# A retention block with two expert layers on one core: each chunk's attention gathered into one piece, and the weight conversion re-portioned around it

## The chip, the cores and the metric

The kernel runs on one core of one Trainium2 chip. The metric is device time in microseconds (us) of one launch. Three runs of the kernel before gave 1004.82, 1004.98 and 1005.65 us, median 1004.98.

## The reference: what is computed

Inputs are float64 arrays in two expert layers and float32 arrays in the attention; the kernel splits each wide number into a high and a low half and multiplies in three passes.

```python
# attention: batch 4, heads 8, 768 steps, head size 64; gamma is one number per head
for t in range(S):
    state = gamma * state + outer(k[:, :, t], v[:, :, t])
    y[:, :, t] = scale * q[:, :, t] @ state
x = y as (3072, 512)
h = x @ w_in                                   # 512 -> 2048
x = where(h > 0, h, exp(min(h, 0)) - 1) @ w_out  # 2048 -> 512
h = max(x @ w1, x @ w2, x @ w3)                # 512 -> 768
out = h @ w_out2                               # 768 -> 512
```

## The kernel before

**Chunks and blocks.** The 3072 tokens are 24 chunks of 128 (`NCHUNK`); four chunks make one block of 512 tokens (`BLK`, `CB = 4`), so there are six blocks, counted from 0. Six chunks make one sequence (`NCH`): chunks 12 and 18 begin one and need no old state, chunks 17 and 23 end one and need no new state.

**A chunk's attention** has these parts. `scores(c)` (L154): sixteen TensorE (PE) passes into two PSUM tiles `sc`. `mask(c)` (L166): VectorE (DVE) multiplies both by the decay mask into `a`. `mix(c)`, the values: `xo` from the old state and the decayed queries `qd` (L205), then from `a` and v (L209); ScalarE (ACT) copies `xo` to `xh` (L217). `rest(c)` (L222): DVE makes the low half `xl`. `update(c)`: `up` from the decayed keys `kd` and v (L182), then DVE decays the old state into the new one (L189, both operands in SBUF) and adds `up` from PSUM (L192); in a sequence's first chunk it only copies `up` (L187). `prep(c)` makes `qd` (L130) and `kd` (L138), from chunk 8 on by GpSimd (POOL). `qd`, `kd` and `a` have one buffer each from chunk 12 on.

**The first expert layer** runs through `seq`, steps of a block b and a slice f of 128 of the 2048 hidden units. A step issues `h1` of the next slice (12 matmuls into a PSUM tile `hp`, L339), then `o1` of its own (12 matmuls into four `acc` tiles, L371). Behind `hp` stands a chain: ACT exp (L346), ACT relu (L347), DVE max (L348, reads `hp`), ACT cast to `gh` (L349), DVE subtraction to `gl` (L352); `o1` reads `gh` and `gl` one step later. `hp`, `xo`, `up` and `sc` share four PSUM buffers, `ps_h`. After a block's last slice `x2_out` empties `acc` (ACT L403, DVE L405).

**Weight conversion** of the second expert layer is cut into portions by `pump(k)`, which lets the generator `conversion` go on for k credits: DVE L280, L290, L291, L298, L306, L307 and ACT L283, L301 for each half tile, and DVE L427, L430, L435 with ACT L433 for the sums of weights. From step `split` (32) on, `h1` itself pumps 2 credits ahead of L352 and 2 behind it, and each step pumps more at its end.

**The order** on PE, DVE, ACT and SP is the order in which the code issues the work; POOL's is left to a scheduler. In blocks 2 to 4 the step f with f % 4 == 1 issues `values(c)` for the next block's chunk ahead of its `h1`, and the step with f % 4 == 2 issues `following(c)`, the next chunk's scores and mask. These are chunks 12 to 23.

Of the kernel before, what the change touches and what calls it, by code (L numbers as in the profile page):

```python
# [40 lines left out]
def kernel(ctx: ExitStack, tc: tile.TileContext, qkv0, qkv, wa, wb, dmask, qdec, cols, out):  # L41
# [10 lines left out]
    ps_h = ctx.enter_context(tc.tile_pool(name="ps_h", bufs=4, space=bass.MemoryType.PSUM))  # L52
# [21 lines left out]
    CB = BLK // P  # L74
# [70 lines left out]
    def scores(c, pool, tag):  # L145

        if c >= NCHUNK:
            return
        x = raw_t[c]
        sc = sc_t[c] = [pool.tile([P, NPAIR, P], F32, tag=tag, name="sc") for _ in range(2)]  # L150
        for p in range(NPAIR):
            for r in range(2):
                h = slice(r * D, (r + 1) * D)
                nc.tensor.matmul(sc[r][:, p, :], x[h, p, 1, :], x[h, p, 0, :], start=p == 0, stop=p == NPAIR - 1)  # L154

    def mask(c):
        if c >= NCHUNK:
            return
        sc = sc_t.pop(c)
        a = st_t[c][2]  # L160
        if a is None:
            a = at.tile([P, 2, NPAIR, P], F32, tag="a", name="a")
        else:
            a = a.rearrange("t r p i -> t r p i")
        for r in range(2):
            nc.vector.tensor_tensor(  # L166
                out=a[:, r], in0=sc[r], in1=dmask_sb.rearrange("j (p r) i -> j r p i", r=2)[:, r], op=ALU.mult
            )
        a_t[c] = a
# [3 lines left out]
    def update(c, pool, tag):  # L173

        kd = st_t[c][1]
        if c % NCH == NCH - 1:
            return
        v = raw_t[c][:, :, 3, :].rearrange("t p (r d) -> t p r d", r=2)
        up = pool.tile([P, NPAIR, D], F32, tag=tag, name="up")
        for p in range(NPAIR):  # L180
            for r in range(2):
                nc.tensor.matmul(  # L182
                    up[r * D:(r + 1) * D, p, :], kd[:, p, r, :], v[:, p, r, :], start=p == 0, stop=p == NPAIR - 1
                )
        new, old = state[c % 2], state[1 - c % 2]
        if c % NCH == 0:
            nc.vector.tensor_copy(new, up)  # L187
        else:
            nc.vector.tensor_tensor(  # L189
                out=new, in0=old, in1=cols_sb[:, H:H + NPAIR].unsqueeze(2).to_broadcast([P, NPAIR, D]), op=ALU.mult  # L190
            )
            nc.vector.tensor_tensor(out=new, in0=up, in1=new, op=ALU.add)  # L192

    def mix(c, pool, tag, then=None):
        v = raw_t[c][:, :, 3, :].rearrange("t p (r d) -> t p r d", r=2)
        qd = st_t[c][0]
        a = a_t.pop(c)
        xo = xo_t[c] = pool.tile([P, NPAIR, P], F32, tag=tag, name="xo")
        first = True
        if c % NCH != 0:  # L200
            old = state[1 - c % 2]
            for p in range(NPAIR):
                for r in range(2):
                    h = slice(r * D, (r + 1) * D)
                    nc.tensor.matmul(xo[h, p, :], old[h, p, :], qd[h, p, :], start=p == 0, stop=False)  # L205
            first = False
        for p in range(NPAIR):
            for r in range(2):
                nc.tensor.matmul(  # L209
                    xo[r * D:(r + 1) * D, p, :], v[:, p, r, :], a[:, r, p, :],  # L210
                    start=first and p == 0, stop=p == NPAIR - 1,
                )
        if then:
            then(c, pool, tag)
        del raw_t[c], st_t[c]
        b, t0 = divmod(c * P, BLK)
        nc.scalar.copy(x_t[b][0][:, :, t0:t0 + P], xo)  # L217

    def rest(c):
        b, t0 = divmod(c * P, BLK)  # L220
        xh, xl = x_t[b]
        nc.vector.tensor_tensor(  # L222
            out=xl[:, :, t0:t0 + P], in0=xo_t.pop(c), in1=f32(xh[:, :, t0:t0 + P]), op=ALU.subtract
        )
# [95 lines left out]
    NB = NT // BLK  # L320

    def new_x(b):
        x_t[b] = (
            xpool.tile([P, KDM, BLK], F32R, tag="xh", name="xh"),
            xpool.tile([P, KDM, BLK], F32R, tag="xl", name="xl"),
        )
# [159 lines left out]
    def pump(k):  # L486

        credit[0] += k
        while credit[0] > 0:
            credit[0] -= next(pending, 1000000)  # L490
# [111 lines left out]
    def values(c):  # L602

        b = c // CB
        if b not in x_t:
            new_x(b)
        load(c)
        load(c + 1)
        load(c + 2)
        if c + 1 < NCHUNK:  # L610
            prep(c + 1)
        mix(c, ps_h, "h", update)
        rest(c)

    def following(c):
        scores(c + 1, ps_h, "h")
        mask(c + 1)

    def pool(name, bufs, **k):
        return ctx.enter_context(tc.tile_pool(name=name, bufs=bufs, reuse_waits="tile", **k))  # L620
# [158 lines left out]
    for i, (b, f, f0, f1) in enumerate(seq):  # L779
        if i < 2:  # L780
            continue
        if (b, f0) in units:
            done = (units[b, f0] - 1) * CB + f // CB
            if f % CB == 1:
                values(done)
            elif f % CB == 2:
                following(done)
        c = EARLY
        if split - 5 <= i < split - 1 or i == split:
            k = c + min(i - split + 5, 4)  # L790
            scores(k, ps_h, "h")
            mask(k)
        if i == split - 2:
            part_t[b] = []
            for m in range(KDM):
                o = f32(dpool.tile([P, BLK], (I32, F32)[m % 2], tag="tm"[m % 2], name="tm"[m % 2]))
                nc.sync.dma_start(out=o, in_=x2d[m, :, b * BLK:(b + 1) * BLK])
                part_t[b].append(o)
        if i == split - 1:
            o1(b, f, f0, f1)  # L800
            x2_out(b, f0, f1, False)
            h1(*seq[i + 1][:2])
            prep(c + 4)
            continue
        if i == len(seq) - 5:
            pump(100000)
            reopen()
            load_sums(0)
            sums(0)
            for k in XORD:  # L810
                later.append(lambda k=k: split_sum(0, k))
        if i == len(seq) - 4:
            fetch_set(loads[-1][0])
        if i == len(seq) - 3:
            fetch_set(loads[-1][1])
            fetch_set(loads[-1][2])
        if i + 1 == len(seq):
            break
        if i < split and n < 2 * KFF:
            h1(*seq[i + 1][:2], [(cv_high, n)], [(cv_bits, n + 1)] if n + 1 < 2 * KFF else [])  # L820
        elif i >= len(seq) - 5:
            h1(*seq[i + 1][:2], [], [(catch_up, 1)])
        elif i > split:
            h1(*seq[i + 1][:2], [(pump, 2)], [(pump, 2)])
        else:
            h1(*seq[i + 1][:2])
        o1(b, f, f0, f1)
        if f == f1 - 1:
            x2_out(b, f0, f1, f1 < KFF and (b, f0) != (0, 10))
        if i >= len(seq) - 5:  # L830
            catch_up(2)
        elif i > split:
            pump(1 if b < NB - 1 and f % CB in (1, 2) else 4)
        for at_step, k in ((11, c), (8, c + 1), (7, c + 2), (5, c + 3), (2, c + 4)):
            if i == split - at_step:
                load(k)
        if i == split - 7:
            prep(c)
        if split - 5 <= i < split - 1:
            if i == split - 5:  # L840
                new_x(2)
            end(c + i - split + 5)
            rest(c + i - split + 5)
        for at_step, k in ((5, 1), (4, 2), (3, 3)):
            if i == split - at_step:
                prep(c + k)
        if i < split and n < 2 * KFF:
            cv_low(n)
            if n + 1 < 2 * KFF:
                cv_rest(n + 1)  # L850
            n += 1
            if i == 2:
                cv_high(n)
                cv_bits(n + 1)
                cv_low(n)
                cv_rest(n + 1)
                n += 1
        while i < split and done_f < n // 2:
            if done_f >= RES:
                keep(done_f)  # L860
            done_f += 1
        for c, g in ((0, i + 1), (1, i)):
            if g < len(seq):
                b, f = seq[g][:2]
                if b >= 2 and f >= KFF - NRING and b + 1 < NB:
                    fetch(RES + f - (KFF - NRING), c)
                if b == 2 and 1 <= f <= NRING:
                    fetch(RES + f - 1, c)
                if b >= 2 and RES <= f < KFF - NRING:
                    fetch(f + NRING, c)  # L870
# [12 lines left out]
    for v, (s, j) in enumerate(visits):  # L883
# [3 lines left out]
        if 2 <= v < 2 + KF2:  # L887
            f = v - 2
# [88 lines left out]
```

## Time and profile before

| | |
|---|---|
| median of three runs | 1004.98 us |
| the profiled execution's own time | 1005.29 us |
| its span | 1003.5 us |
| PE busy | 984.8 us (98%) |
| DVE busy | 690.7 us (69%) |
| ACT busy | 352.9 us (35%) |
| POOL busy | 35.9 us (4%) |
| granted TensorE clock | 1.00 throughout |

The span is the profiled execution from its first to its last instruction; 1.79 us of its own time lie around it. "Busy" of PE counts a matmul up to its modelled end, so the rows are read by the starts of matmuls. A row of the timeline gives start, length, engine, line, operation, tiles, shape and count; in brackets stands idle time ahead of it and what ended it. PE's records count each attention matmul twice.

### The profile page before, as it was taken

How to read it: one execution, taken by the hardware profiler on the slowest of the kernel's cores; microseconds unless marked ns; L12 is line 12 of the kernel's file. 1: busy time of each engine (PE TensorE's matmuls, PEld its weight loads, DVE VectorE, ACT ScalarE, POOL GpSimd, SP SyncE). 2: the span in 40 equal slices, each digit the busy share in tenths (PEclk: the TensorE clock that was granted, in tenths of full speed). 3: DMA queues.
4: the chain of work that ended last, by engine and by line, in shares of the span. 5: the costliest groups of instructions: out<-in, count | busy, mean ns of one | idle time of the engine just before them, and what ended most of it. 6: DMA issues, size and time to landing. Idle time of an engine off the chain costs nothing.

```text
span 1003.5 us, 14377 instructions
## 1 busy us (share of the span) xinstructions
PE 984.8 (98%) x5684; PEld 848.0 (85%) x5685; DVE 690.7 (69%) x1190; ACT 352.9 (35%) x630; POOL 35.9 (4%) x31
## 2 busy tenths in 40 slices
PE   7989999999999999999999999999999999999998
PEld 5777888777888888888888788999899989989996
DVE  4889989975576776677776743688658827864771
ACT  4546555422434444444434443311301311130110
POOL 0000000120011100001100000000000000000000
PEclk9999999999999999999999999999999999999999
DMA  9723336876538773696428717983355055204601
GB/s 272 202 83 106 104 127 198 277 218 207 179 98 268 262 256 96 230 314 211 157 85 325 282 54 271 373 322 145 105 177 212 1 185 211 98 22 156 253 1 63
DMA packets 75315, 180.78 MB, mean 180 GB/s; under 512 B 5872, under 2 KB 42736, under 8 KB 71024
## 3 DMA queue, kind: packets, MB, share of 16 engines
q1 hardware_dynamic: 73088, 175.92, 51.6%
q10 hardware_dynamic: 2160, 3.94, 1.1%
q8 instruction: 45, 0.74, 0.3%
q14 instruction: 22, 0.18, 0.1%
HBM read 139.20 MB, written 40.63 MB: 179 GB/s over the span
## 4 chain that ended last, share of the span: by engine, by line
PE 86%; DVE 7%; DMA 4%; ACT 2%; issue 1%; SPq 0%; ACTq 0%; DVEq 0%
PE pp L693 26%; PE hp L339 24%; PE acc L371 23%; PE ac L745 10%; DMA x<-in_qkv 2%; DMA raw<-in_wa 1%; PE xo L209 1%; PE sc L154 1%; PE xo L205 1%; DVE gl L352 1%; DVE e L348 1%; DVE part L388 1%; DVE t L298 1%; ACT gh L349 1%; DVE w L307 1%; DVE m L291 1%
## 5 line engine op out<-in xcount | busy, mean ns | idle before, releaser
L693 PE MATMUL pp<-xs,op 128*128 128x384 f32 x1512 | 267.8, 334 | 0.0
L693 PEld LDWEIGHTS pp<-xs,op 128*128 128x128 f32 x1512 | 263.3, 188 | 3.0
L339 PE MATMUL hp<-xh,w 128*128 128x512 f32 x768 | 248.1, 394 | 4.7 <-DVE state L192 2.5
L371 PE MATMUL acc<-gh,w 128*128 128x512 f32 x768 | 193.9, 391 | 3.1 <-ACT w L301 1.7
L339 PEld LDWEIGHTS hp<-xh,w 128*128 128x128 f32 x768 | 143.7, 188 | 38.1 <-ACT w L301 2.4
L371 PEld LDWEIGHTS acc<-gh,w 128*128 128x128 f32 x768 | 143.0, 188 | 36.4 <-ACT w L301 2.6
L348 DVE SCALAR_TENSOR_TENSOR e<-e,hp 128x512 f32<-128x512 f32 x96 | 65.7, 685 | 111.6 <-ACT e L347 111.6
L339 PE MATMUL hp<-xl,w 128*128 128x512 f32 x384 | 141.9, 390 | 0.0
L745 PE MATMUL ac<-w,g 128*128 128x512 f32 x432 | 104.5, 391 | 0.0
L371 PE MATMUL acc<-gl,w 128*128 128x512 f32 x384 | 102.7, 389 | 0.0
L346 ACT ACTIVATE e<-hp 128x512 f32<-128x512 f32 x96 | 57.2, 596 | 103.0 <-PE hp L339 102.9
L745 PEld LDWEIGHTS ac<-w,g 128*128 128x128 f32 x432 | 80.6, 188 | 14.9
L349 ACT CAST gh<-e 128x512 fp32r<-128x512 f32 x96 | 59.7, 622 | 89.0 <-DVE e L348 89.0
L709 ACT COPY u<-pp 128x384 f32<-128x384 f32 x36 | 17.3, 480 | 201.2 <-PE pp L693 140.9
L371 PEld LDWEIGHTS acc<-gl,w 128*128 128x128 f32 x384 | 72.1, 188 | 15.1
L339 PEld LDWEIGHTS hp<-xl,w 128*128 128x128 f32 x384 | 72.1, 188 | 14.4
L352 DVE TENSOR_TENSOR gl<-e,gh 128x512 fp32r<-128x512 f32 x96 | 68.5, 713 | 19.7 <-ACT gh L349 16.9
L701 DVE TENSOR_TENSOR c<-pp,u 128x384 f32<-128x384 f32 x96 | 52.8, 553 | 36.1 <-PE pp L693 35.7
L347 ACT ACTIVATE e<-e 128x512 f32<-128x512 f32 x96 | 60.7, 633 | 3.1
L283 ACT ACTIVATE t<-t 128x512 int32<-128x512 int32 x56 | 35.4, 633 | 54.1 <-DVE t L280 54.1
L301 ACT CAST w<-t 128x512 fp32r<-128x512 f32 x56 | 34.8, 621 | 43.4 <-DVE t L298 40.0
L723 DVE TENSOR_TENSOR h<-h,c 128x768 f32<-128x768 f32 x48 | 45.9, 957 | 1.6
(72 smaller groups left out, 817.1 us busy)
## 6 DMA issues: line engine op xcount, KB each, us to landing
op<-opd SPq DMA_DIRECT2D x24, 1792.0 KB, 7.5
w<-kept SPq DMA_DIRECT2D x56, 512.0 KB, 6.7
raw<-in_wa SPq DMA_DIRECT2D x32, 512.0 KB, 3.7
x<-in_qkv SPq DMA_DIRECT2D x24, 512.0 KB, 6.2
raw<-in_wb SPq DMA_DIRECT2D x24, 512.0 KB, 4.4
x<-in_qkv SPq DMA_DIRECT2D x80, 128.0 KB, 5.3
opd<-w SPq DMA_DIRECT2D x9, 1024.0 KB, 8.0
kept<-w SPq DMA_DIRECT2D x14, 512.0 KB, 5.6
```

The source lines that it names most:

```text
L283: nc.scalar.activation(t, t, ACTF.Relu, scale=8.0, bias=-896.0 * 2 ** 23)
L339: nc.tensor.matmul(hp, w[:, pw, kk * P:(kk + 1) * P], x[px][:, kk, :], start=k == 0, stop=k == len(order) - 1,)
L346: nc.scalar.activation(e, hp, ACTF.Exp)
L347: nc.scalar.activation(e, e, ACTF.Relu, scale=-1.0, bias=1.0)
L348: nc.vector.scalar_tensor_tensor(out=e, in0=e, scalar=-1.0, in1=hp, op0=ALU.mult, op1=ALU.max)
L349: nc.scalar.copy(gh, e)
L352: nc.vector.tensor_tensor(out=gl, in0=e, in1=f32(gh), op=ALU.subtract)
L371: nc.tensor.matmul(acc_t[b][m], w[:, p[0], m * P:(m + 1) * P], g[p[1]], start=f == f0 and p == first, stop=f == f1 - 1 and p == final,)
L693: nc.tensor.matmul(o, ws[i][:, pw, kk * P:(kk + 1) * P], xs[i][:, px, kk, :], start=k == 0, stop=k == 5)
L701: nc.vector.tensor_tensor(out=out, in0=a, in1=c, op=ALU.add)
L723: nc.vector.tensor_tensor(out=h_t[s, p][i], in0=h_t[s, p][i], in1=c[i], op=ALU.max)
L745: nc.tensor.matmul(ac_t[s, m], g[:, px, m * P:(m + 1) * P], wo_t[f][:, pw, :], start=first and i == 0, stop=final and i == 2,)
```

## The change

In `values`, the update stands ahead of the values, the next chunk's scores stand right behind them, and the mask behind `rest`, followed by two credits of conversion. `following` is gone. The credits at a step's end were 4, 1, 1, 4 for f % 4 = 0, 1, 2, 3 and become 0, 3, 4, 4.

```diff
-        mix(c, ps_h, "h", update)
+        update(c, ps_h, "h")
+        mix(c, ps_h, "h")
+        scores(c + 1, ps_h, "h")
         rest(c)
-
-    def following(c):
-        scores(c + 1, ps_h, "h")
         mask(c + 1)
+        pump(2)
...
             if f % CB == 1:
                 values(done)
-            elif f % CB == 2:
-                following(done)
...
         elif i > split:
-            pump(1 if b < NB - 1 and f % CB in (1, 2) else 4)
+            pump((0, 3, 4, 4)[f % CB] if b < NB - 1 else 4)
```

PE, block 2, around chunk 14: `up` is the state's increment, `xo` the values, `sc` the scores of chunk 15, `acc` belongs to `o1` and `hp` to `h1`. Before:

```order
L371 MATMUL acc<-gl,w 128x512 x4
L205 MATMUL xo<-qd,state_93 64x128 x8
L209 MATMUL xo<-a,x 64x128 x8
L182 MATMUL up<-x,kd 64x64 x8
L339 MATMUL hp<-xh,w 128x512
...
L371 MATMUL acc<-gl,w 128x512 x4
L154 MATMUL sc<-x 128x128 x8
L339 MATMUL hp<-xh,w 128x512
```

and now:

```order
L371 MATMUL acc<-gl,w 128x512 x4
L182 MATMUL up<-x,kd 64x64 x8
L205 MATMUL xo<-qd,state_93 64x128 x8
L209 MATMUL xo<-a,x 64x128 x8
L154 MATMUL sc<-x 128x128 x8
L339 MATMUL hp<-xh,w 128x512
```

The update moved ahead of the values, the scores moved one step forward, and the next `hp` is the fifth PSUM tile counted from `up` instead of the second: it takes `up`'s buffer.

DVE, the same place (`t`, `m`, `raw`, `w` are conversion, `e` and `gl` the chain behind `hp`). Before:

```order
L348 SCALAR_TENSOR_TENSOR e<-e,hp 128x512
L430 TENSOR_TENSOR w<-w 128x256
L352 TENSOR_TENSOR gl<-e,gh 128x512
L306 TENSOR_SCALAR t<-t 128x512
L307 SCALAR_TENSOR_TENSOR w<-m,t 128x512
L435 TENSOR_TENSOR w<-w 128x256
L280 TENSOR_SCALAR t<-raw 128x512
L427 TENSOR_TENSOR w<-w 128x256
L189 TENSOR_TENSOR state_92<-state_93,cols_sb 128x256
L192 TENSOR_TENSOR state_92<-up,state_92 128x256
L222 TENSOR_TENSOR xl<-xo,xh 128x4x128
```

and now:

```order
L348 SCALAR_TENSOR_TENSOR e<-e,hp 128x512
L352 TENSOR_TENSOR gl<-e,gh 128x512
L430 TENSOR_TENSOR w<-w 128x256
L435 TENSOR_TENSOR w<-w 128x256
L189 TENSOR_TENSOR state_92<-state_93,cols_sb 128x256
L192 TENSOR_TENSOR state_92<-up,state_92 128x256
L222 TENSOR_TENSOR xl<-xo,xh 128x4x128
L166 TENSOR_TENSOR a<-sc,dmask_sb 128x512 x2
```

Between L348 and L189 there were seven instructions and are now three; the masks follow at once.

POOL, `kd` and `qd` of chunks 13 to 16. Before:

```order
L130 TENSOR_TENSOR qd<-x,qdec_sb 128x512
L138 TENSOR_TENSOR kd<-x,cols_sb 128x512
L130 TENSOR_TENSOR qd<-x,qdec_sb 128x512
L138 TENSOR_TENSOR kd<-x,cols_sb 128x512
L130 TENSOR_TENSOR qd<-x,qdec_sb 128x512
```

and now:

```order
L138 TENSOR_TENSOR kd<-x,cols_sb 128x512 x2
L130 TENSOR_TENSOR qd<-x,qdec_sb 128x512
L138 TENSOR_TENSOR kd<-x,cols_sb 128x512
L130 TENSOR_TENSOR qd<-x,qdec_sb 128x512
L138 TENSOR_TENSOR kd<-x,cols_sb 128x512
```

`kd` of the next chunk, whose buffer the update sets free, now stands ahead of `qd`, whose buffer L205 sets free.

## Rows read from the trace of the kernel before

**Rows 1.** The page, busy time: engine, us, share of the span, instructions.

```profile
PE 984.8 (98%) x5684; PEld 848.0 (85%) x5685; DVE 690.7 (69%) x1190; ACT 352.9 (35%) x630; POOL 35.9 (4%) x31
```

**Rows 2.** Busy time by stretch, blocks 2 to 4: PE, PEld, DVE, ACT, POOL, clock.

```profile
245.00:550.00 305.00, 305.00 (x1848) 248.53 (x1847) 210.72 (x394) 131.24 (x233) 24.56 (x19) 1.00 0.63 209
```

**Rows 3.** Timeline of PE around chunk 14 and the steps behind it.

```profile
303.35 1.09 PE L205 MATMUL xo<-qd,state 64*64 64x128 f32 x16
...
305.86 0.50 PE L339 MATMUL hp<-xh,w 128*128 128x512 f32 x1
...
308.72 1.98 PE L371 MATMUL acc<-gh,w 128*128 128x512 f32 x8
...
311.53 1.16 PE L154 MATMUL sc<-x 64*128 64x128 f32 x16
312.62 0.50 PE L339 MATMUL hp<-xh,w 128*128 128x512 f32 x1
...
318.20 0.39 PE L339 MATMUL hp<-xh,w 128*128 128x512 f32 x1
...
320.92 0.39 PE L371 MATMUL acc<-gh,w 128*128 128x512 f32 x1
```

**Rows 4.** Timeline of PE and DVE at chunk 9, where the update already stands first.

```profile
218.27 0.69 PE L182 MATMUL up<-x,spare 128*64 128x64 f32 x16
...
220.93 1.16 PE L154 MATMUL sc<-x 64*128 64x128 f32 x16
...
222.38 0.42 DVE L192 TENSOR_TENSOR state<-up,state 128x256 f32<-128x256 f32 x1
...
222.86 0.50 PE L339 MATMUL hp<-xh,w 128*128 128x512 f32 x1 [0.77 <-DVE state L192]
```

**Rows 5.** Waits of PE: who, for whom, us in total, times, longest.

```profile
PE hp L339 <- DVE state L192: 2.5, 3, 1.4
```

**Rows 6.** Timeline of DVE, then of POOL, at chunk 8.

```profile
209.17 1.37 DVE L352 TENSOR_TENSOR gl<-e,gh 128x512 fp32r<-128x512 f32 x1
210.46 1.48 DVE L189 TENSOR_TENSOR state<-state,cols_sb 128x256 f32<-128x256 f32 x1
...
208.57 1.42 POOL L138 TENSOR_TENSOR kd<-x,cols_sb 128x512 f32<-128x512 f32 x1 [4.90 <-DMA x<-in_qkv]
209.95 1.71 POOL L130 TENSOR_TENSOR qd<-x,qdec_sb 128x512 f32<-128x512 f32 x1
```

**Rows 7.** Timeline of PE and POOL: `kd` behind an update (chunk 12), `qd` at chunk 9.

```profile
253.66 0.64 PE L182 MATMUL up<-x,kd 128*64 128x64 f32 x16
...
254.44 1.04 POOL L138 TENSOR_TENSOR kd<-x,cols_sb 128x512 f32<-128x512 f32 x1 [1.79 <-PE up L182]
...
220.12 1.27 POOL L130 TENSOR_TENSOR spare<-x,qdec_sb 128x512 f32<-128x512 f32 x1 [8.46 <-PE xo L205]
```

**Rows 8.** Timeline of DVE and ACT in an undisturbed step of block 2.

```profile
322.41 0.69 DVE L348 SCALAR_TENSOR_TENSOR e<-e,hp 128x512 f32<-128x512 f32 x1 [1.46 <-ACT e L347]
...
324.08 0.68 DVE L352 TENSOR_TENSOR gl<-e,gh 128x512 fp32r<-128x512 f32 x1
324.69 0.42 DVE L430 TENSOR_TENSOR w<-w 128x256 f32<-128x256 f32 x1
325.57 0.43 DVE L435 TENSOR_TENSOR w<-w 128x256 fp32r<-128x256 f32 x1 [0.47 <-ACT w L433]
...
323.13 0.62 ACT L349 CAST gh<-e 128x512 fp32r<-128x512 f32 x1 [0.76 <-DVE e L348]
325.13 0.41 ACT L433 CAST w<-w 128x256 fp32r<-128x256 f32 x1 [1.38 <-DVE w L430]
```

**Rows 9.** Timeline of PE and ACT where block 5 begins.

```profile
552.99 0.39 PE L339 MATMUL hp<-xh,w 128*128 128x512 f32 x1
...
556.25 2.10 PE L371 MATMUL acc<-gh,w 128*128 128x512 f32 x8 [0.38 <-ACT w L301]
...
557.38 0.59 ACT L346 ACTIVATE e<-hp 128x512 f32<-128x512 f32 x1
```

## The prediction

> **What bounds the kernel now.** I read the page's busy times first: PE is busy for 984.8 of 1003.5 us [rows 1]. In the table by stretch the part that the change touches, blocks 2 to 4, shows PE busy in all of 305 us at the full clock, while DVE works 211 us and ACT 131 us [rows 2]. So PE's own order of work is the path there: time can be won only by shortening what PE runs, and is lost wherever another engine makes it wait. The third view is PE's timeline, from which two things are read: what a switch between large matmuls and the small ones of attention costs, and which waits PE has where the new order already exists, in chunks 8 to 10.
>
> **What PE saves.** Twelve matmuls of `h1` or `o1` take 320.92 - 318.20 = 2.72 us [rows 3]. The twelve ahead of an attention part take 311.53 - 308.72 = 2.81, those behind one 308.72 - 305.86 = 2.86: leaving costs 0.09, coming back 0.14. Before, a chunk is left and entered twice: 0.09 + 2.51 (303.35 to 305.86, values and update) + 0.14, then 0.09 + 1.09 (311.53 to 312.62, scores) + 0.14 = 4.06 us. In the new order update and values take 220.93 - 218.27 = 2.66 [rows 4], 0.15 more than 2.51, because the inner changes of shape differ. The sum is 0.09 + 2.66 + 1.09 + 0.14 = 3.98. Chunks 13 to 16 and 19 to 22 so save 0.08 each, 0.64. Chunks 12, 17 and 18 lack either values from the state or the update, so inner changes fall away, and they save up to 0.09 + 0.14 = 0.23 each, 0.69. Chunk 23 has no next scores and saves nothing. **PE saves 1.3 us in all**; the bounds are 0.9 (0.08 for all eleven) and 2.5 (0.23 for all).
>
> **What the credits do.** Over blocks 2 to 4 the steps' ends and `values` now hand out 13 credits in four steps instead of 10, and conversion is done when block 4 is, where it used to reach into block 5. DVE has room: 305 - 211 us [rows 2]. At the start of block 5 twelve matmuls take 556.25 - 552.99 = 3.26 instead of 2.72, since ACT casts a weight (L301) ahead of emptying `acc` [rows 9]. With less conversion there **0.5 us** should go; bounds are 0 and 0.54. The conversion's DMAs keep their number and come earlier; SP's x loads stand at the same step, a whole chunk (some 26 us) ahead of use, so I price both at nothing.
>
> **The new wait.** `hp` of the step behind the piece takes the buffer of `up`, which is free when L192 has read it. Behind that matmul all of PE's queue waits. The same layout stands at chunks 8 to 10, and there PE waited for L192 three times out of three, 2.5 us together [rows 5], [rows 4] for one. I count from the piece's first matmul. `hp` is due at 2.66 + 1.09 = 3.75, and starts 0.06 after L192's end (222.80 to 222.86). L192 takes 0.42, its forerunner L189 as long when undisturbed, 0.10 lies between. So L189 must begin by 2.75.
>
> What delays it is POOL. While POOL runs L138 or L130, a DVE instruction whose inputs are all in SBUF stands still: L352 began inside L138 and ended 0.55 after it (210.54 against 209.99); L189 began inside L130 and ended 0.28 after it (211.94 against 211.66) [rows 6]. Undisturbed they take 0.68 [rows 8] and 0.42. So POOL stops one such instruction per operation. In the new order POOL's `kd` stands ahead of its `qd` and begins 0.78 after an update does [rows 7], with the first small matmul's delay 0.83. It takes between 1.04 [rows 7] and 1.42 [rows 6], I take 1.22; `qd` takes 1.27 [rows 7] to 1.71 [rows 6], I take 1.5, the middle in both, as DVE competes in every chunk. POOL is thus in the way from 0.83 to 3.55, just when L189 is due.
>
> Chunk 14 in full: `o1` starts 2.81 ahead of the piece, L348 1.49 after that [rows 3, 8], so at -1.32. L349 starts 0.72 later and takes 0.62, to 0.02; L352 starts at 0.07. L430 follows 0.61 later at 0.68, ACT's L433 at 1.12, L435 at 1.56 [rows 8]. That falls into `kd` (to 2.05), so L435 ends at 2.33. L189 falls into `qd` (to 3.55) and ends at 3.83; L192 runs to 4.35; `hp` starts at 4.41 instead of 3.75: **0.7 us lost**.
>
> The other chunks go by what still stands ahead of L189 at 0.83. With two such instructions (13, 19, 21) both of POOL's operations are used up by them, L189 begins near 3.8 and `hp` is 1.1 late. In 15 they are L290 and the longer L291: 1.3. Chunk 16 has no `kd` to make, but its chain starts late: behind a block's last slice ACT empties `acc` first, and at block 5 L346 began at 557.38 where 552.99 + 2.72 + 0.20 = 555.91 was due [rows 9], 1.5 late. That moves L189 behind `qd` (which begins 1.85 after the piece [rows 4, 7]): 1.1. In 20 L433, L435, L280 and L283 stand behind the copies as well, four operations of about 0.4 with their hand-overs; L346 is 2.5 late and six DVE instructions remain ahead of L189: 2.7. Chunk 22 has no `kd`, and L189 starts near 1.7, ahead of `qd`: 0. Chunks 12, 17, 18 and 23 have no L189. **Sum: 1.1 + 0.7 + 1.3 + 1.1 + 1.1 + 2.7 + 1.1 = 9.1 us.** Bounds: 0, when every L189 begins by 2.75, and about 13, when POOL takes its longer 1.42 and 1.71 (0.4 more in seven chunks, 3) and chunk 15 loses a second wide instruction. Many starts lie within 0.1 us of POOL's, which is why I keep the middle value. The three early pieces, at 0.8 on average, would give 6.7 for eight.
>
> Here the Trainium skill can be weighed (SBUF — State Buffer, "Who interferes with whom"): the side that starts first holds the shared ports for its whole instruction and the other "fully blocks". By that page a stopped DVE instruction would run its whole length after POOL's, 0.42 where the trace shows 0.28; that would add 0.14 in seven chunks, 1.0 us. The measurement decides.
>
> **The sum.** -1.3 - 0.5 + 9.1 = +7.3 us. The profiled execution's own time is 1005.29 (span 1003.5), which gives 1012.6; it lies 0.3 above the median of the runs, 1004.98, so I forecast **1012.3**.
>
> **Rivals.**
> 1. *Nothing is stopped.* If DVE clears its queue early enough that L189 itself is what `kd` stops, it ends near 2.3 and L192 near 2.9, in time. It decides at L435 in chunk 14, which would have to begin before 0.83, 0.7 earlier than reckoned, and likewise elsewhere. For it: the step ahead of `values` now has no credits at its end, and DVE is free for a third of the time. Against it: ACT's cast stands between L430 and L435, and all three early pieces waited. Time: 1005.0 - 1.3 - 0.5 = 1003.2, not slower.
> 2. *Half of it.* The queue is some 0.4 us ahead of my reckoning, so that one instruction fewer is stopped in 13, 15, 19 and 21, each then costing 0.7, and L346 is on time in 16 and 20 (0.3 each): 0.7 x 5 + 0.6 = 4.1. Time: 1004.98 - 1.8 + 4.1 = 1007.3.
> 3. *DVE falls behind.* With 13 credits L346 comes 1.5 late or more in most pieces, as at block 5 [rows 9]; chunks 13 to 16 and 19 to 21 then all cost about what 20 does, 2.7 x 7 = 19. Time: 1022. Against it: only steps that follow a block's end show such lateness so far.
>
> **How the numbers follow.** About 0.2% (2 us) is what a measurement of this kernel can tell from no change. The forecast has 0.60, rival 1 0.14, rival 2 0.14, rival 3 0.12. Rival 1 lies within 0.2% or, with PE's upper bound of 2.5 saved, below it: 0.05 faster and 0.09 the same; rival 2 adds 0.03 to the same. So faster 0.05, same 0.12, slower 0.83. The forecast with its bounds runs from about 1008 to 1016; the range goes down to 1005.0 to take in rival 2 and up to 1017.0 for a mild form of rival 3, and leaves out rival 1.
>
> **What would show it.** Right: PE's waits name L192 behind `hp` in six or seven of chunks 13 to 16 and 19 to 21, each row following a piece; L189 or the instruction ahead of it reads 1.2 to 1.6 us; chunk 20 is the worst; DVE has no conversion in block 5; twelve matmuls at block 5's start take about 2.72. Pieces without a wait run 3.98 from large to large. Wrong: `hp` following `sc` without idle time (rival 1), or waits at `acc` for `gl` and `gh` across blocks 2 to 4 (rival 3).

## The result and the profile after

The changed kernel takes **1015.03 us** in the median (1014.52 to 1015.81), the kernel before on the same chip 1005.32 (1004.82 to 1005.86): a ratio of 1.010, 95% interval 1.0088 to 1.0113. The profiled execution's own time is 1014.52 us, its span 1012.6, which is 9.1 more than before.

The page's busy times, and the line of `h1`'s matmuls among its costliest groups (matmuls, their busy time and mean ns, then the idle time just before them and what ended most of it):

```profile
PE 986.2 (97%) x5685; PEld 850.0 (84%) x5685; DVE 688.5 (68%) x1190; ACT 354.5 (35%) x630; POOL 35.4 (3%) x31
...
L339 PE MATMUL hp<-xh,w 128*128 128x512 f32 x768 | 247.9, 394 | 12.2 <-DVE state L192 9.9
```

Against [rows 1] PE is busy 1.4 us longer and the span is 9.1 longer: most of the loss is idle time of PE. The list of PE's waits of the changed kernel says whom it waited for (in total, times, longest):

```profile
PE hp L339 <- DVE state L192: 9.9, 10, 2.6
```

The three early waits of [rows 5] have become ten. The table by stretch, for blocks 2 to 4 as in [rows 2] and then two microseconds at a time around chunk 20 (columns: stretch, its length, busy us of PE, PEld, DVE, ACT, POOL, the clock, DMA):

```profile
245.00:550.00 305.00, 296.93 (x1808) 242.40 (x1807) 214.35 (x408) 132.98 (x235) 24.77 (x20) 0.99 0.63 213
...
464.00:466.00 2.00, 1.24 (x20) 0.97 (x16) 1.97 (x4) 1.40 (x3) 0.55 (x1) 1.00 0.16 47
466.00:468.00 2.00, 0.12 (x1) 0.12 (x2) 1.86 (x5) 0.00 (x0) 0.00 (x0) 1.00 0.65 178
468.00:470.00 2.00, 2.00 (x7) 1.59 (x8) 1.95 (x4) 0.00 (x0) 0.00 (x0) 0.71 0.96 259
470.00:472.00 2.00, 2.00 (x7) 1.54 (x6) 0.00 (x0) 0.00 (x0) 0.00 (x0) 0.50 0.20 67
472.00:474.00 2.00, 2.00 (x10) 1.66 (x9) 0.18 (x1) 1.23 (x2) 0.00 (x0) 0.94 0.00 0
```

PE, for which the table of [rows 2] shows no idle time in these 305 us, now stands for 8.1 of them. And in the lower rows is something that the prediction did not have: behind the longest wait the granted clock is 0.5, which is 1.2 GHz, and for a while PE is busy at half speed.

**A usual piece.** Timeline of chunk 14, the one that the prediction worked out, on PE, DVE and POOL (start, length, what; in brackets the idle time before and who ended it):

```profile
305.12 0.69 PE L182 MATMUL up<-x,kd 128*64 128x64 f32 x16
...
307.78 1.16 PE L154 MATMUL sc<-x 64*128 64x128 f32 x16
309.39 0.50 PE L339 MATMUL hp<-xh,w 128*128 128x512 f32 x1 [0.44 <-DVE state L192]
...
306.73 0.66 DVE L435 TENSOR_TENSOR w<-w 128x256 fp32r<-128x256 f32 x1 [0.53 <-ACT w L433]
307.31 1.49 DVE L189 TENSOR_TENSOR state<-state,cols_sb 128x256 f32<-128x256 f32 x1
308.91 0.42 DVE L192 TENSOR_TENSOR state<-up,state 128x256 f32<-128x256 f32 x1
...
305.96 1.15 POOL L138 TENSOR_TENSOR kd<-x,cols_sb 128x512 f32<-128x512 f32 x1 [24.03 <-PE up L182]
307.07 1.45 POOL L130 TENSOR_TENSOR qd<-x,qdec_sb 128x512 f32<-128x512 f32 x1
```

POOL's `kd` begins 0.84 behind the update's first matmul and runs to 307.11; L435 begins inside it and ends 0.28 after it. `qd` follows and runs to 308.52; L189 begins inside it, ends 0.28 after it, and takes 1.49 us where it needs 0.42. L192 is done at 309.33 and `hp` starts 0.06 later. The scores take 1.09 from their start when nothing waits, so `hp` was due at 308.87 and is 0.5 late.

**The worst piece.** Chunk 20, the first piece of block 4, right behind a block's end, on PE, ACT and DVE:

```profile
464.08 1.16 PE L154 MATMUL sc<-x 64*128 64x128 f32 x16
467.88 0.50 PE L339 MATMUL hp<-xh,w 128*128 128x512 f32 x1 [2.64 <-DVE state L192]
...
461.36 0.63 ACT L283 ACTIVATE t<-t 128x512 int32<-128x512 int32 x1 [0.83 <-DVE t L280]
461.90 0.58 ACT L346 ACTIVATE e<-hp 128x512 f32<-128x512 f32 x1
...
463.17 0.69 DVE L348 SCALAR_TENSOR_TENSOR e<-e,hp 128x512 f32<-128x512 f32 x1 [1.84 <-ACT e L347]
463.78 1.06 DVE L427 TENSOR_TENSOR w<-w 128x256 f32<-128x256 f32 x1
...
467.40 0.42 DVE L192 TENSOR_TENSOR state<-up,state 128x256 f32<-128x256 f32 x1
```

L346 belongs to an `hp` that ended at 458.44, where `acc` begins. It starts 3.46 us later instead of 0.20, so 3.3 late, because ACT first does conversion (L283 waits for DVE's L280). DVE idles 1.84 us for it and has seven instructions left to do before L192.

**Block 5.** Timeline of PE there, the same step as in [rows 9]: twelve matmuls now take 565.59 - 562.87 = 2.72 us where they took 3.26 and more.

```profile
562.87 0.39 PE L339 MATMUL hp<-xh,w 128*128 128x512 f32 x1
...
565.59 1.98 PE L371 MATMUL acc<-gh,w 128*128 128x512 f32 x8
```

**The balance.** To leave out the start of the kernel, which comes out differently from run to run, I take the stretch from the first attention matmul of chunk 12 to that of chunk 23 on PE's timeline: 534.49 - 252.73 = 281.76 us before, 544.13 - 253.38 = 290.75 after, 9.0 more. The pieces lose by waits, each the time from its first score to the next `hp` less 1.09: chunk 13 1.42, 14 0.51, 15 1.32, 16 0.43, 19 0.56, 20 2.71, 21 1.15, 22 none: **8.1**. The low clock costs 1.6, stops at the starts of blocks 3 and 4 cost 0.5 more than before, fewer switches save 1.3: together 8.9, with 0.1 left open. Outside the stretch chunk 23 loses 0.2, block 5 gains 0.7, and the stretch began 0.65 later, with code ahead of it that the change does not touch.

### The profile page after: what moved, and what is told of

Read it like the earlier page. It is cut to its first block, busy times and chain, and to the rows that moved or that the text cites. A ratio compares the mean times of both kernels' runs of the same rounds, so it can differ in the third digit from the quotient of the medians.

```text
span 1012.6 us, 14391 instructions
## 1 busy us (share of the span) xinstructions
PE 986.2 (97%) x5685; PEld 850.0 (84%) x5685; DVE 688.5 (68%) x1190; ACT 354.5 (35%) x630; POOL 35.4 (3%) x31
## 4 chain that ended last, share of the span: by engine, by line
PE 65%; DVE 4%; ACT 2%; DMA 1%; issue 0%; DVEq 0%; ACTq 0%
PE pp L693 26%; PE hp L339 15%; PE acc L371 13%; PE ac L745 10%; DMA w<-kept 1%; DVE gl L352 1%; DVE w L427 1%; ACT e L347 1%; ACT e L346 0%; DVE e L348 0%; PE sc L154 0%; DVE state L189 0%; PE xo L209 0%; ACT gh L349 0%; PE xo L205 0%
## 5 line engine op out<-in xcount | busy, mean ns | idle before, releaser
L339 PE MATMUL hp<-xh,w 128*128 128x512 f32 x768 | 247.9, 394 | 12.2 <-DVE state L192 9.9
L371 PE MATMUL acc<-gh,w 128*128 128x512 f32 x768 | 193.9, 391 | 3.0 <-ACT w L301 1.6
L339 PEld LDWEIGHTS hp<-xh,w 128*128 128x128 f32 x768 | 144.4, 189 | 45.8 <-DVE state L192 10.3
L371 PEld LDWEIGHTS acc<-gh,w 128*128 128x128 f32 x768 | 143.2, 188 | 36.2 <-ACT w L301 2.2
L348 DVE SCALAR_TENSOR_TENSOR e<-e,hp 128x512 f32<-128x512 f32 x96 | 65.9, 687 | 120.9 <-ACT e L347 120.6
L339 PE MATMUL hp<-xl,w 128*128 128x512 f32 x384 | 142.5, 391 | 0.0
L371 PE MATMUL acc<-gl,w 128*128 128x512 f32 x384 | 102.7, 389 | 0.0
L346 ACT ACTIVATE e<-hp 128x512 f32<-128x512 f32 x96 | 57.1, 595 | 114.4 <-PE hp L339 113.9
L352 DVE TENSOR_TENSOR gl<-e,gh 128x512 fp32r<-128x512 f32 x96 | 70.4, 733 | 24.4 <-ACT gh L349 21.0
L339 PEld LDWEIGHTS hp<-xl,w 128*128 128x128 f32 x384 | 72.4, 189 | 14.8
L371 PEld LDWEIGHTS acc<-gl,w 128*128 128x128 f32 x384 | 72.1, 188 | 15.2
L347 ACT ACTIVATE e<-e 128x512 f32<-128x512 f32 x96 | 60.7, 632 | 3.0
L283 ACT ACTIVATE t<-t 128x512 int32<-128x512 int32 x56 | 35.4, 632 | 50.6 <-DVE t L280 50.5
```

Source lines behind the costliest of these rows:

```text
L283: nc.scalar.activation(t, t, ACTF.Relu, scale=8.0, bias=-896.0 * 2 ** 23)
L339: nc.tensor.matmul(hp, w[:, pw, kk * P:(kk + 1) * P], x[px][:, kk, :], start=k == 0, stop=k == len(order) - 1,)
L346: nc.scalar.activation(e, hp, ACTF.Exp)
L347: nc.scalar.activation(e, e, ACTF.Relu, scale=-1.0, bias=1.0)
L348: nc.vector.scalar_tensor_tensor(out=e, in0=e, scalar=-1.0, in1=hp, op0=ALU.mult, op1=ALU.max)
L352: nc.vector.tensor_tensor(out=gl, in0=e, in1=f32(gh), op=ALU.subtract)
```

## The experiments

The stretch is the one just described; before it takes 281.76 us, after 290.75. Waits are the list's row "PE hp <- DVE state" of L192 (three of the times, 2.3 to 2.5 us, are the early ones of [rows 5]). Times are medians, ratios against the kernel before with their 95% interval.

| run | us | ratio | stretch, us | waits for L192 |
|---|---|---|---|---|
| order_only | 1034.59 | 1.0296 (1.0281 to 1.0312) | 310.81 | 21.7 in 11 |
| credits_only | 1005.44 | 1.0003 (0.9993 to 1.0012) | 282.20 | 2.3 in 3 |
| scores_later | 1006.58 | 1.0013 (1.0005 to 1.0022) | 283.55 | 2.3 in 3 |
| prep_vector | 1007.23 | 1.002 (1.0011 to 1.0029) | 285.21 | 4.3 in 4 |
| early_decay | 1010.25 | 1.005 (1.0034 to 1.0065) | 287.01 | 6.7 in 7 |
| fill_wait | 1012.2 | 1.0075 (1.0058 to 1.0091) | 289.04 | 8.1 in 10 |
| prep_vector_light | 1005.92 | 1.0009 (0.9997 to 1.0021) | 283.07 | 4.0 in 4 |
| values_first | 1008.69 | 1.0029 (1.0014 to 1.0044) | 284.62 | 2.3 in 3 |
| combined | 1005.02 | 0.9994 (0.9983 to 1.0005) | 281.48 | 2.3 in 3 |
| combined_pool | 1005.47 | 0.9996 (0.9987 to 1.0006) | 281.72 | 3.0 in 4 |

The theory is that of the prediction: in the new order `hp` takes `up`'s buffer one piece later and waits until L192 has read it, and L192 is late because POOL stops DVE's all-SBUF instructions. Its rivals: the credits do the harm, or the length of DVE's and ACT's queue does, whatever POOL does.

**1. The two halves of the change, each alone.** `order_only` is the change without its credits, `credits_only` the credits without the new order:

```diff
 # order_only, against before
-        mix(c, ps_h, "h", update)
+        update(c, ps_h, "h")
+        mix(c, ps_h, "h")
+        scores(c + 1, ps_h, "h")
         rest(c)
-
-    def following(c):
-        scores(c + 1, ps_h, "h")
         mask(c + 1)
...
-            elif f % CB == 2:
-                following(done)
 # credits_only, against before
         rest(c)
+        pump(2)
...
-            pump(1 if b < NB - 1 and f % CB in (1, 2) else 4)
+            pump((0, 3, 4, 4)[f % CB] if b < NB - 1 else 4)
```

> The changed kernel with the credits of before (4, 1, 1, 4, none behind the mask). Theory: hp behind the piece waits for L192, and L192 waits for what stands ahead of it on VectorE; the new credits keep that queue short. With the old credits L192 should end as late after the piece's start as it did before, 5.7 to 7.2 us, where 3.7 is due: 2 to 3.5 us lost in each of eight chunks, some 20 us, so about 1024 us or more, if TensorE's clock falls in several of these waits. Rival (the credits do the harm, they overload VectorE in blocks 2 to 4): with the old credits the time is that of before less 1.3, about 1004.

> The kernel before with the new credits alone (0, 3, 4, 4, and two behind the values). Theory: PE never waits for L192, since up's buffer goes to a later hp; the stop at the start of block 5 goes (0.5 to 0.7 us), so 1004.6, within 0.2% of before. Rival (the credits do the harm): 1010 or more.

The order does the harm, all of it, and much more without the credits, whose 0 in the step ahead of the piece keeps conversion out of DVE's way: in chunk 14 of `order_only` seven instructions stand between L348 and L189, as before the change, instead of three. `order_only`'s list of waits, and two microseconds of its table by stretch, behind one of its waits:

```profile
PE hp L339 <- DVE state L192: 21.7, 11, 3.4
...
PE hp L339 <- DVE state L187: 2.0, 1, 2.0
```

```profile
284.00:286.00 2.00, 2.00 (x6) 1.54 (x6) 0.54 (x1) 0.00 (x0) 0.00 (x0) 0.50 0.73 247
```

Every piece from chunk 13 to 22 waits but that of chunk 17, and at five places the clock falls to 0.5 behind the wait. The nine waits lose 22.2 us and the five falls some 1.5 each, which is nearly all of the 29 us by which the stretch is longer. The credits alone change nothing that can be measured: block 5's stop goes, but the starts of blocks 3 and 4 stop 0.3 and 0.15 us longer, and `hp` behind chunk 23 waits 0.34 for a weight's DMA.

**2. The same order without the shared buffer's haste.** `scores_later` is the changed kernel with the scores and the mask back in a step of their own:

```diff
         mix(c, ps_h, "h")
-        scores(c + 1, ps_h, "h")
         rest(c)
-        mask(c + 1)
         pump(2)
+
+    def following(c):
+        scores(c + 1, ps_h, "h")
+        mask(c + 1)
...
+            elif f % CB == 2:
+                following(done)
```

> The changed kernel with the scores and the mask of the next chunk moved back by one step; the update stays first and the credits stay new. Theory: only with the scores in the piece does the next hp come round to up's buffer; here it takes another, and no wait for L192 is left behind the piece. PE pays the second interruption again, 4.06 + 0.15 per chunk, 1.2 us over before, less 0.7 at block 5: about 1005.8. Rival (putting the update first does the harm): near 1013.

No piece waits for L192, although POOL's operations and the update's place are those of the changed kernel. `hp` behind the values no longer needs `up`'s buffer so soon. It is 0.8 us above what was expected, and chunk 23 alone accounts for 0.5 of that: behind its values PE loses 0.76 us for a kept weight's DMA, where the changed kernel loses 0.24.

**3. Without POOL.** `prep_vector` gives `kd` and `qd` to VectorE, behind the mask:

```diff
-        pool = nc.vector if early else nc.gpsimd
+        pool = nc.vector if early or c > EARLY + CB else nc.gpsimd
...
-        if c + 1 < NCHUNK:
-            prep(c + 1)
         update(c, ps_h, "h")
...
         mask(c + 1)
+        if c + 1 < NCHUNK:
+            prep(c + 1)
```

> The changed kernel with qd and kd of chunks 13 to 23 made on VectorE behind the mask and not on GpSimd, so that GpSimd does nothing in blocks 2 to 4. Theory: with no GpSimd operation to stop VectorE, L189 begins by 2.4 us after the piece's start in chunks 13 to 15, 19, 21 and 22, so no wait there; chunks 16 and 20 (late ACT behind a block's end) keep 0.1 and 1.4. VectorE has 1.4 us more per chunk, behind the mask where it has room. About 1005 us. Rival (VectorE's queue alone makes L192 late): the waits stay, 1013 to 1016.

Its list of waits, and its timeline of DVE at chunk 14:

```profile
PE hp L339 <- DVE state L192: 4.3, 4, 2.0
```

```profile
305.31 0.42 DVE L435 TENSOR_TENSOR w<-w 128x256 fp32r<-128x256 f32 x1 [0.53 <-ACT w L433]
305.65 0.42 DVE L189 TENSOR_TENSOR state<-state,cols_sb 128x256 f32<-128x256 f32 x1
306.18 0.42 DVE L192 TENSOR_TENSOR state<-up,state 128x256 f32<-128x256 f32 x1
```

The same instructions, in the same order, take 0.42 instead of 0.66 and 1.49, and six of the seven new waits are gone, though DVE now has more to do. So POOL makes them. The seventh, chunk 20, stays at 2.1 us where 1.4 was expected, and the clock falls behind it; this is where 1007.2 instead of 1005 comes from. Of the 8.1 us of waits POOL thus makes 6.0; in chunk 20 its part is 0.6, and the rest is L346's lateness with the queue behind it.

**4. Which instruction is stopped.** `early_decay` is the changed kernel, POOL included, with L189, now in a function `decay` (not shown), issued a chunk ahead:

```diff
...
-            nc.vector.tensor_tensor(
-                out=new, in0=old, in1=cols_sb[:, H:H + NPAIR].unsqueeze(2).to_broadcast([P, NPAIR, D]), op=ALU.mult
-            )
+            if c <= EARLY + CB:
+                decay(c)
             nc.vector.tensor_tensor(out=new, in0=up, in1=new, op=ALU.add)
...
         mask(c + 1)
+        decay(c + 1)
         pump(2)
```

> The changed kernel, but from chunk 13 on the decay of the state (L189) is issued on VectorE right behind the mask of the chunk before, a whole chunk ahead, so that only L192 is left behind the update; credits, piece and GpSimd's kd and qd stay. Theory (GpSimd stops one all-SBUF instruction of VectorE per operation, and in each chunk the last one stopped is L189 or the one ahead of it): where L189 itself was stopped by qd (chunks 14, 16, 19) hp waits no longer; where other instructions are stopped first (13, 15, 20, 21) only the 0.5 us of L189 and its hand-over go. Losses of about 1.0, 0, 0.85, 0, 0, 2.2 and 0.7, together 4.7 instead of 8.1: 1011.6 us, the list of waits naming L192 seven times or fewer for about 6 us instead of 9.9. Rival (the wait is the length of VectorE's queue, whichever instruction stands in it, and L189 merely goes elsewhere): the wait shrinks by L189's undisturbed 0.42 us in each of the seven chunks, 2.9 us, and about evenly: 1012.1 us with 14, 16 and 19 keeping 0.1 to 0.2 each and 13, 15 and 21 0.7 to 1.0; the two differ in whether 14 and 19 vanish and no DVE instruction of over 1.2 us stands right ahead of L192 in 16 and 19.

The losses are 0.88 (chunk 13), 0, 0.80, 0, 0, 2.17 and 0.63, together 4.5. These sizes are the theory's, but they do not rule the rival out: every piece loses about 0.5 us less, or all that it lost, and 0.5 is L189's own 0.42 with a hand-over of 0.10. What parts the two is where the addition (L192) ends, counted from the piece's start: in chunk 14 at 2.60 instead of 4.21, in 16 at 2.56 instead of 4.13, in 19 at 2.64 instead of 4.26. That is 1.6 us earlier, the length of the stopped L189 with the hand-over; in 13, 15, 20 and 21, where L189 itself was not stopped, it ends 0.5 earlier. This is the theory's division. Its timeline of DVE at chunk 13 and at chunk 14, then of PE at chunk 14 (L198 is here the addition that is L192 elsewhere, L358 is L352, L433 is L427, L441 is L435, L345 is L339):

```profile
279.45 1.53 DVE L358 TENSOR_TENSOR gl<-e,gh 128x512 fp32r<-128x512 f32 x1
280.90 1.49 DVE L433 TENSOR_TENSOR w<-w 128x256 f32<-128x256 f32 x1
282.31 0.41 DVE L198 TENSOR_TENSOR state<-up,state 128x256 f32<-128x256 f32 x1
...
306.37 0.66 DVE L441 TENSOR_TENSOR w<-w 128x256 fp32r<-128x256 f32 x1 [0.53 <-ACT w L439]
306.95 0.41 DVE L198 TENSOR_TENSOR state<-up,state 128x256 f32<-128x256 f32 x1
...
307.42 1.16 PE L154 MATMUL sc<-x 64*128 64x128 f32 x16
308.52 0.50 PE L345 MATMUL hp<-xh,w 128*128 128x512 f32 x1
```

In chunk 14 one instruction (L441) meets `kd`, and with L189 away none that matters meets `qd`. In chunk 13 two others stand there and use both up, and only L189's own half microsecond is won.

**5. The clock.** `fill_wait` runs the 16 scores of chunk 21 three times into the same tiles, in the time in which PE would stand:

```diff
-        for p in range(NPAIR):
+        for p in list(range(NPAIR)) * (3 if c == 21 else 1):
```

> The changed kernel, in which the 16 score matmuls of chunk 21 are run three times into the same tiles, so that inside the wait of chunk 20 (2.64 us of an idle PE) TensorE works 2.2 us more; nothing else differs and the added work lies in the time that hp waits anyway. Theory (the clock fell to 0.5 behind this wait because TensorE stood idle in it): the granted clock stays at 1.0 behind chunk 20, the twelve matmuls of hp take 2.8 us instead of 4.4, and the kernel is 1.6 us shorter: 1013.4 us although it does more work. Rival (the fall has another cause, or the repeated scores only lengthen the path): the clock falls at the same place, or the time is 1015.0 to 1017.

PE's timeline behind chunk 20 and the table by stretch there:

```profile
466.12 2.95 PE L154 MATMUL sc<-x 64*128 64x128 f32 x48
469.92 0.50 PE L339 MATMUL hp<-xh,w 128*128 128x512 f32 x1 [0.85 <-DVE state L192]
```

```profile
468.00:470.00 2.00, 1.15 (x21) 0.96 (x17) 1.86 (x5) 0.00 (x0) 0.00 (x0) 1.00 0.52 141
470.00:472.00 2.00, 2.00 (x9) 1.65 (x10) 1.99 (x4) 0.00 (x0) 0.00 (x0) 1.00 0.77 189
```

From the first score to `hp` it is 3.80 us in both kernels, so the 2.2 us of added work are hidden. The clock stays at 1.0, and the twelve matmuls behind, 4.44 in the changed kernel, take their usual time. The stretch is 1.7 us shorter. At this place idling was the cause of the fall. The median is 2.8 us below the changed kernel's, more than that: the stretches explain 1.7, and the rest lies outside them.

**6. Chunk 20, and what beats the changed kernel.** `prep_vector_light` hands out no credits at a block's last step; `values_first` has in addition values, update, scores in this order and L222 ahead of the state; `combined` joins `prep_vector`, `early_decay` and no credits at f % 4 = 3; `combined_pool` is that with `kd` and `qd` left on POOL.

```diff
 # prep_vector_light, against prep_vector
-            pump((0, 3, 4, 4)[f % CB] if b < NB - 1 else 4)
+            pump((0, 3, 4, 0 if f == KFF - 1 else 4)[f % CB] if b < NB - 1 else 4)
 # values_first, against prep_vector_light (state_of holds L187 to L192)
-        update(c, ps_h, "h")
-        mix(c, ps_h, "h")
+        mix(c, ps_h, "h", update)
         scores(c + 1, ps_h, "h")
         rest(c)
+        state_of(c)
         mask(c + 1)
 # combined, against prep_vector with early_decay
-            pump((0, 3, 4, 4)[f % CB] if b < NB - 1 else 4)
+            pump((0, 3, 4, 0)[f % CB] if b < NB - 1 else 4)
```

> kd and qd on VectorE behind the mask, as in the run prep_vector, and in addition no credits at the end of a block's last step (f = 15), whose conversion stood between the copies out of acc and the Exp (L346) of the next step; those 12 credits are given out in block 5. Theory (chunk 20 waits because L346 comes 3.3 us late behind a block's end, not because of GpSimd): the wait for L192 at chunk 20, 2.1 us, and the fall of the clock behind it, 1.6 us, go, and so does most of the stop at block 4's first acc matmuls: prep_vector's 1007.2 less 3 to 3.7, 1003.5 to 1004.2 us, 1 to 1.5 below the kernel before. Rival (chunk 20 is late for the length of VectorE's own chain ahead of L192): 1007 stays, with hp waiting 1.5 us or more at chunk 20.

> As prep_vector_light, but in the piece the values stand first, then the update, then the next scores, so that hp takes the PSUM buffer of the values (xo) instead of that of the update, and VectorE runs rest (the reader of xo) ahead of the state's two instructions. Theory (what counts is only how early the buffer that hp takes is read out; the inner order values, update is 0.15 us shorter than update, values): xo is written 2.05 us into the piece, its cast takes 0.6 and rest 0.7, so hp can start at 3.5 where the scores end at 3.6 to 3.7; no new wait, and eight chunks save 0.15 us each: 1.2 us under prep_vector_light, 1002.5 us. Rival (xo has two readers on two engines and its release comes later than that of up): hp waits for rest by 0.3 us or more in each of eleven chunks, and the kernel is 2 us or more slower than prep_vector_light, 1006 us.

> The changed kernel with three things together: kd and qd on VectorE behind the mask, the decay (L189) issued a chunk ahead, and credits of 0, 3, 4, 0 at the steps' ends, so that no cast of conversion stands on ScalarE ahead of the Exp (L346) whose chain precedes a piece. Theory (the piece itself saves TensorE 1.3 us, and every wait for L192 came either from GpSimd or from L346 held back by conversion handed out at the step's end): none of the eight pieces waits for L192, the clock does not fall behind one, and the time is the kernel before less 1.3, plus the 0.5 to 0.9 us of stops at the start of blocks 3 and 4 that the other credits also showed: 1004.6 to 1005.0 us, and 1003.9 if those stops go with the conversion. Rival (the late L346 is inherent to where the piece stands): chunks 19 or 20 still wait 1.5 us or more and the time is 1006 or above.

> As combined, but kd and qd stay on GpSimd where the changed kernel has them. Theory: with L346 on time, GpSimd can still hold up whichever all-SBUF instructions stand ahead of L192, so pieces with two of them behind L348 wait 0.6 to 0.9 us each and those with one or none wait nothing: 0 to 4 us above combined, about 1006.5; instructions of 256 columns that normally take 0.42 us read 1.2 to 1.5 in those pieces. Rival (once L346 is on time GpSimd does not matter): within 0.5 us of combined.

`prep_vector_light`: chunk 20's wait and the fall of the clock are gone, as the theory wanted, but the median is 1005.9, since with conversion shifted by four credits chunk 19 waits 1.7 us. Its timeline of PE and ACT there:

```profile
426.64 2.11 PE L371 MATMUL acc<-gh,w 128*128 128x512 f32 x8
...
435.06 0.50 PE L339 MATMUL hp<-xh,w 128*128 128x512 f32 x1 [1.66 <-DVE state L192]
...
429.08 0.41 ACT L433 CAST w<-w 128x256 fp32r<-128x256 f32 x1 [2.49 <-DVE w L430]
429.39 0.59 ACT L346 ACTIVATE e<-hp 128x512 f32<-128x512 f32 x1
```

It is the same cause at another place: a cast of conversion (L433) that waits for DVE stands ahead of L346 and makes it 2.5 us late. So chunk 20 was no matter of the block's end alone; any conversion handed out at the end of the step ahead can do it.

`values_first` went the rival's way, but only at three chunks (16, 19 and 20: the list names L230 three times with 4.0 us; chunk 18 loses 0.1), and the reason at chunks 16 and 20 is neither theory's; in chunk 19 it is the cast ahead of L346 again. Its timeline of ACT and PE at chunk 20 (here L225 is the cast L217, L230 is L222, L347 is L339):

```profile
463.26 0.59 ACT L225 CAST xh<-xo 128x512 fp32r<-128x512 f32 x1 [3.67 <-DMA x2d<-o]
...
464.63 0.50 PE L347 MATMUL hp<-xh,w 128*128 128x512 f32 x1 [1.85 <-DVE xl L230]
```

The first cast of a block goes into a buffer of `xpool` out of which the DMA still writes the output of the block before; through `xo`'s buffer this now holds up `hp`. Where nothing waits the inner order saves 0.11 us of the 0.15: chunks 13 and 14 are 25.63 apart, against 25.74 in `prep_vector_light`.

`combined` has no piece that waits. Its list of waits (the three early ones alone), and its timeline of PE at chunk 14 and at block 3's start (L377 is L371, L345 is L339):

```profile
PE hp L345 <- DVE state L198: 2.3, 3, 1.3
```

```profile
304.06 1.16 PE L154 MATMUL sc<-x 64*128 64x128 f32 x16
305.15 0.50 PE L345 MATMUL hp<-xh,w 128*128 128x512 f32 x1
...
351.99 1.33 PE L377 MATMUL acc<-gh,w 128*128 128x512 f32 x4 [0.63 <-DVE o L411]
```

It is 10 us faster than the changed kernel and as fast as the one before: the stretch is 281.48 against 281.76. The 1.3 us that fewer switches save are there, but block 3's start now stops 1.1 us (L377, for DVE's copies out of `acc`) where it stopped 0.25 before, and 0.2 more goes in small amounts that I did not follow up. Block 5's start still stops 0.9. `combined_pool` comes within 0.45 us of it, as the rival had it, but this is luck in part: POOL still delays chunk 18 by 0.81 and chunk 19 by 0.59, 1.4 us together, and the start of block 3 happens to stop 0.16 us instead of 1.1. The two `hp` (L194 is L187):

```profile
408.85 0.50 PE L345 MATMUL hp<-xh,w 128*128 128x512 f32 x1 [0.74 <-DVE state L194]
...
435.17 0.50 PE L345 MATMUL hp<-xh,w 128*128 128x512 f32 x1 [0.52 <-DVE state L198]
```

`early_decay` and `combined_pool` differ in the credits alone, and the losses fall from 4.5 to 1.4 us with POOL's operations in place. A late L346 is not what POOL needs, though: in the changed kernel it was late in chunks 15 (0.6), 16 (0.9) and 20 (3.3) only, and on time in 13, 14, 19 and 21. What counts is which instructions still stand ahead of L192 when POOL begins. So two things make the large loss: POOL's two operations in the piece, and instructions that they can stop ahead of L192. These credits without the early L189 were not run. No version beat the kernel before by more than a measurement tells.

## Why the prediction was right

**Right, by its mechanism.** It forecast 1012.3 within 1005.0 to 1017.0 and gave slower 0.83; measured are 1015.03. Runs 1 to 4 show the mechanism and not just the sum: without the order no loss, without the shared buffer no wait, without POOL no stopped instruction, and without L189 in the queue an L192 that ends 1.6 us earlier in exactly those chunks in which L189 was stopped.

**Step by step.** *What PE saves*: 1.3 forecast; the inner lengths came out to the hundredth, and chunks 13 and 14 in `prep_vector` are 25.74 us apart where they were 25.82 apart before, 0.08 as priced. *What the credits do*: 0.5 forecast at block 5, 0.7 measured; but the sentence that DVE has room missed the other side, 0.5 us of longer stops at the starts of blocks 3 and 4 and 0.2 at chunk 23, so that the credits alone are worth nothing. *The new wait*: 9.1 forecast, 8.1 measured, by chunk (forecast, measured): 13 1.1 and 1.42, 14 0.7 and 0.51, 15 1.3 and 1.32, 16 1.1 and 0.43, 19 1.1 and 0.56, 20 2.7 and 2.71, 21 1.1 and 1.15, 22 0 and 0. Where the count of stopped instructions was right (13, 14, 15, 21), what is left is mostly POOL's own length: in chunk 13 `kd` and `qd` took 1.46 and 1.72 instead of the 1.22 and 1.5 reckoned with, in 14 1.15 and 1.45. In two chunks the count was wrong. In 16 L346 was 0.9 late and not 1.5, so that L189 began inside `qd` and not behind it. In 19, DVE (POOL's `kd` runs from 435.75 to 436.95, `qd` from 436.92 to 438.36):

```profile
435.64 0.42 DVE L435 TENSOR_TENSOR w<-w 128x256 fp32r<-128x256 f32 x1
435.98 1.26 DVE L427 TENSOR_TENSOR w<-w 128x256 f32<-128x256 f32 x1
437.16 1.49 DVE L189 TENSOR_TENSOR state<-state,cols_sb 128x256 f32<-128x256 f32 x1
```

L435 began 0.11 ahead of `kd` and got through, so L427 met `kd` and L189 met `qd`, as in chunk 14. In chunk 20 the right sum hides a wrong part: L346 came 3.3 late instead of 2.5, and what stood behind it took less than reckoned. That the waits came out at 8.1 so rests in part on errors that cancel.

**What it missed.** The low clock behind chunk 20, 1.6 us, is no term of the sum; [rows 2] show 1.00 throughout, and nothing in them told what PE's idling would do. The late start of the stretch, 0.65, lies outside the change. These and the stops, less the 1.0 that the waits were overrated, make 1.8 of the 1.9 us between the forecast own time of 1012.6 and the 1014.52 of the profile. The other 0.8 by which the median missed comes from the execution that was profiled: its time was 0.3 above the median of the three runs before and is 0.5 below the median now.

**The page that was weighed.** The Trainium skill (SBUF — State Buffer, "Who interferes with whom") says that the side which comes second is fully blocked. Here the trace agrees in part: L189, 0.42 long when undisturbed, begins 0.24 after `qd` does and ends only 0.28 after it. What I had derived from that page, a whole 0.42 behind POOL's end, did not happen; the sum went by the rows, rightly.

**The rivals.** *Nothing is stopped* fell: seven pieces wait. *Half of it* is 4 us short in all, but it was the nearer one in 16 (0.3 against 0.43 measured) and in 19 (0.7 against 0.56), where one instruction fewer was stopped ahead of L189, as it says. *DVE falls behind* would have been the case without the credits: `order_only` shows losses of 1.9 to 3.5 us in nearly every piece.

## What to carry to other kernels

When matmuls are joined into one piece to save switches, count the buffers of the pool from the first tile of the piece to the first large matmul behind it: whoever must read that tile out now has only the piece's length to do so, and whatever that engine still has in its queue, or is stopped by, comes on top. The 1.3 us that the switches gave were less than one bad piece cost. Work handed out in spare time belongs behind the chain that the next piece waits for, not ahead of it: a cast of 0.4 us that waits for another engine made the chain 2.5 us late.

## What was not expected of the hardware

- **A wait of PE can cost more than its length.** Behind chunk 20's wait of 2.64 us the granted clock was 0.5 (1.2 GHz) for 3.4 us (worked out from the table by stretch above), and twelve matmuls took 4.44 us instead of 2.86. With the wait filled by repeated work it stayed at 1.0. Not every long wait did it: in `prep_vector` one of 2.0 us did, in `early_decay` the one of chunk 20 (2.2 us lost) did, in `values_first` one of 1.85 did not, and in `order_only` two pieces that lost 2.4 and 2.5 us did not while one that lost 2.0 did.
- **A granted clock of 0.95 in the rows went with no longer large matmuls.** In `order_only`'s profile it is 0.95 in undisturbed steps, and twelve large matmuls take 2.72 us there as at 1.0; behind the five waits after which it fell to 0.5 they took 4.15 to 4.45. Sixteen small ones of L205 took 1.04 us instead of 1.02. The reason is open.
- **An instruction that POOL has stopped ends sooner after it than its own length**: 0.28 us for 256 columns (0.42 long), as [rows 6] had it, in chunk 14 twice over, so the first part of it seems to be done while it stands. This rests on the ends that the profile gives for POOL, which are rough, and was not tested.
